# Seven products of a tile: two PSUM chains of one bank each, read between the products, in place of four banks read in four groups

## Chip, cores and metric

The kernel runs on one core of a Trainium2 chip. The metric is device time in microseconds (us) of one execution; before the change its median is 845.22 us over three runs (844.39 to 845.75).

## Reference, cut to what matters

For 8 sequences of 3008 tokens with 256 channels, the first half is a spectral filter (FFT along the sequence, a complex 256x256 matrix, a soft threshold, the inverse FFT). Its result, 24064 tokens by 256, goes through a two-layer block:

```
def _moe_ref(x, w_in, w_out, s, b):      # w_in 256 x 2048, w_out 2048 x 256
    h = x @ w_in
    r = np.maximum(h, 0.0)
    g = s * (r * r) + b
    return (g @ w_out).astype(np.float32)
```

The change concerns the last product alone. Since s and b are scalars, the kernel computes `out = s * (r*r) @ w_out + bias`, where `bias` is b times the column sums of w_out, held in the tile `bias_bc`.

## The kernel before, in words

**Stages.** Each sequence (batch) passes through the filter in stages of small matmuls: stage 1 (tiles x, u), stages 2 and 3 (xf, s, ring, v), stage 4 (vs to yt). The stages' matmuls are cut into units, and `plan` (L1072 to L1118) hangs the units of later batches between the matmuls of the two-layer block of an earlier one. The main loop (L1121 to L1133) runs over token tiles `ti` of up to 512 tokens and, in each, over 16 slots `mc`. A slot emits its planned units, two matmuls of `first_mm` (L847: 512 columns each, into a two-bank tile psh), and then seven or eight matmuls of the *second* layer of the tile before. Every second slot, ScalarE applies the relu to a psh pair (L867, rt<-psh) and ScalarE or VectorE squares it into gt (L877 or L880).

**Who evacuates and squares.** A planner in Python keeps a running load for ScalarE and VectorE (`work`, `act_first`, L175 to L189): each emitted operation adds its cost to its engine, and a free choice (an evacuation in `evac`, a square in `first_mm`) goes to the engine that would be done first. An operation on VectorE that costs less shifts later choices. Each engine executes its own queue in order; the framework adds the waits.

**The seven products.** For 22 of the tiles (`seven`, L1063) the second layer is not done with 8 blocks but with 7 (Winograd's form). The 512 tokens are two halves i, the 2048 hidden channels two halves k (even and odd mc), the 256 outputs two halves j. With a for the squares and B for w_out, VectorE forms s1 = a21+a22 (`s_op` 1), a21 := a11-a21 (`s_op` 3), a11 := a11-s1 (`s_op` 2), and a DMA issued on GpSimd adds the new a11 to a12 (`s_op` 4, L969). Each is done per half q of the hidden dimension. `make_t` (L369) has made four sums T of blocks of w_out. The products, by the numbers that the changed code uses, are

```
1: a11 B11   2: a12 B21   4: a22 T3   5: s1 T0   6: (a11-s1) T1   7: (a11-a21) T2   3: (a12+a11-s1) B22
top left = 1+2;  bottom left = 1+6+7+4;  bottom right = 1+6+7+5;  top right = 1+6+5+3
```

Products 1 and 2 need a11 and a12 as they were, 6 needs `s_op` 2 of both halves, 7 needs `s_op` 3, 5 needs `s_op` 1. A product is 16 matmuls of 128x128 (2 token blocks by 8 channel blocks); the tile's 112 matmuls fill 16 slots of seven. In the first 18 of the 22 tiles products 1 and 2 are interleaved by halves of the channels, in the last four (`alone`, L1045) three are.

**Banks and readout before** (`seven_mms`, L979). The order is 1 2 4 5 6 7 3. A tile takes four banks of 512 floats, with products 1 and 2 in the two halves of one, 4 in one, 5 and 6 in one, 7 and 3 in one. In the first 18 tiles they come from the pool psa with two buffers in turn, in the last four alternately from psa and psf (`sum_bank`, L211). `leave` (L1016) reads them on VectorE in four groups: after 1 and 2 two scalar_tensor_tensor (L1008, `add`) and one tensor_tensor (L1026) that makes a second running sum in `zz` with the other bias; after 4 one; after 5 and 6 one of 256 and one of 512 elements; after 7 and 3 three. The results go to two ost tiles, and SP's queue stores all four at the end. Tiles that are not of the seven kind go through `second_mms` (L918): eight matmuls of 256 columns a slot, one bank for two blocks of 128 tokens, one VectorE readout (L941).

**Order on VectorE around it.** `s_op` 2 and 1 of q=0 and q=1 stand in slot 2 of the products, 3 of q=1 in slot 3, 2 of q=1 in slot 4; `s_op` 1 and 3 of q=0 are emitted one tile earlier, in slots 10 and 11 (L1130).

Of the kernel before, what the change touches and what calls it, by code (L numbers as in the profile page):

```python
# [10 lines left out]
F32 = mybir.dt.float32  # L11
# [85 lines left out]
def kernel(  # L97
# [48 lines left out]
    apool = ctx.enter_context(tc.tile_pool(name="psa", bufs=2, space=bass.MemoryType.PSUM))  # L146
# [66 lines left out]

    def other_bank():
        return apool.tile([P, 512], F32, name="psa", tag="psa")
# [146 lines left out]
    b_21 = cpool.tile([P, P], F32, name="b_21")  # L362
# [6 lines left out]
    def make_t(i):  # L369

        if not T_s:
            nc.vector.tensor_tensor(
                out=b_21, in0=bias_bc[:, P:D], in1=bias_bc[:, 0:P], op=ALU.subtract
            )
            T_s.append(x2pool.tile([P, 4, MC // 2, P], F16, name="T_s", tag="x2"))
# [603 lines left out]
    def seven_mms(ti):  # L979

        tl = tiles[ti]
        size = sub_size(tl)
        hold = {}
        left = [(0, 0), (0, 1), (1, 1), None, (0, 0), (1, 0), (0, 1)]
        firsts = (0, 2, 3, 5)
        T = T_s[0]
        right = [w_block(0, 0), w_block(1, 0), T[:, 3], T[:, 0], T[:, 1], T[:, 2], w_block(1, 1)]

        def mm(n, j, c):

            if n in firsts and j == 0 and c == 0:
                hold["ps"] = sum_bank(ti).rearrange("p (n j e) -> p n j e", n=2, j=2)
            if j == 0 and c == 0:
                hold[n] = hold["ps"][0:size, 0 if n in firsts else 1]
            q, g = divmod(c, 4)
            at = slice(j * size, (j + 1) * size)
            if left[n] is None:
                lhs = sums[(ti, q)][:, g, at]
            else:
                lhs = gts[(ti, q)][:, left[n][0], left[n][1], g, at]  # L1000
            matmul(
                hold[n][:, j], lhs, right[n][:, c],
                start=(n in firsts and j == 0 and c == 0), stop=(c == MC // 2 - 1),
# [3 lines left out]
        def add(out, of, other):  # L1007
            nc.vector.scalar_tensor_tensor(  # L1008
                out=out, in0=of, scalar=s_bc[0:size], in1=other, op0=ALU.mult, op1=ALU.add
            )  # L1010
            work("dve", 0.4)

        def wide(t):
            return t[0:size, 0:P].unsqueeze(1).to_broadcast([size, 2, P])

        def leave(group):  # L1016
            if group == 0:
                hold["z"] = zpool.tile([P, 2, 2, P], F32, name="zz", tag="zz")
            if group in (0, 3):
                hold["o", group] = opool.tile([P, 2, D], F32, name="ost", tag="ost")  # L1020
            z = hold["z"][0:size]
            top = hold["o", 0][0:size]
            if group == 0:
                add(z[:, 0], hold[0], wide(bias_bc))
                add(top[:, :, 0:P], hold[1], z[:, 0])
                nc.vector.tensor_tensor(out=z[:, 1], in0=z[:, 0], in1=wide(b_21), op=ALU.add)  # L1026
                work("dve", 0.34)
            elif group == 1:
                add(z[:, 0], hold[2], z[:, 0])
            elif group == 2:  # L1030
                add(z[:, 1], hold[3], z[:, 1])
                two = hold[4].rearrange("p j e -> p (j e)").unsqueeze(1).to_broadcast([size, 2, D])
                zs = z.rearrange("p h j e -> p h (j e)")
                add(zs, two, zs)
                work("dve", 0.27)
            else:
                for h in range(2):
                    add(hold["o", 3][0:size, :, h * P : (h + 1) * P], hold[5], z[:, h])
                add(top[:, :, P:D], hold[6], z[:, 1])
                for i in range(2):  # L1040
                    for j in range(2):
                        store(tl, 2 * (1 - i) + j, hold["o", 3 * (1 - i)][:, j, :])
# [122 lines left out]
```

## Time and profile before

| what | value |
|---|---|
| median of three runs | 845.22 us (844.39 to 845.75) |
| the profiled execution's own time | 843.5 us |
| its span, first to last instruction | 841.7 us |
| mean granted TensorE clock | 0.999 |
| PE busy | 823.0 us (98% of the span), 7710 matmuls |
| weight loads (PEld) | 599.3 us (71%) |
| VectorE (DVE) busy | 718.2 us (85%), 1120 instructions |
| ScalarE (ACT) busy | 722.1 us (86%), 959 instructions |
| GpSimd (POOL) busy | 87.7 us (10%) |
| readouts of the seven products (L1008 and L1026) | 198 instructions |

How to read it: an engine's busy time is the time in which it had an instruction running. Matmuls overlap each other, so a busy PE may still have waited between two starts. A view of waits gives, for an engine and tile, what ended its idle time. The timeline gives start and length of each instruction, equal neighbours merged, with the idle time ahead of it in brackets.

### The profile page before, as it was taken

Reading aid. Unit: us, or ns where it says so; the run is one execution under the profiler, and the core shown is the slowest. Engines: PE = TensorE matmul, PEld = TensorE weight load, DVE = VectorE, ACT = ScalarE, POOL = GpSimd, SP = SyncE. Lnnn points to the kernel's source line nnn. Section 1 sums busy time; section 2 is a strip of 40 time slices with the busy share of each in tenths; the row PEclk is TensorE's granted clock in tenths of the full one; section 3 lists DMA queues with packets and bytes.
Section 4 is the critical chain, followed back from the end, with each engine's and each line's share of the span. In section 5 each row is a group of like instructions: output and inputs, shape, how many; then the busy total and the mean of one; then the engine's idle time right before and its main releaser. Section 6 shows DMA issues by size and latency. Waiting matters only on the chain.

```text
span 841.7 us, 19681 instructions
## 1 busy us (share of the span) xinstructions
PE 823.0 (98%) x7710; PEld 599.3 (71%) x7710; DVE 718.2 (85%) x1120; ACT 722.1 (86%) x959; POOL 87.7 (10%) x116
## 2 busy tenths in 40 slices
PE   8999999999999999999999999999999999999997
PEld 7857767777677767776677666777667767767765
DVE  5988989998898888888888888788889888879885
ACT  5998988998899988988899888889879898788882
POOL 4550001110010001100010000100001000001000
PEclk9999999999999999999999999999999999999999
DMA  8954587356873478436773458614565253513322
GB/s 199 180 152 102 124 195 193 63 104 151 202 177 66 107 173 215 105 90 143 188 184 70 96 137 206 168 53 108 131 175 142 51 109 99 144 45 76 71 64 62
DMA packets 116959, 107.70 MB, mean 128 GB/s; under 512 B 12806, under 2 KB 100874, under 8 KB 115522
## 3 DMA queue, kind: packets, MB, share of 16 engines
q1 hardware_dynamic: 102498, 80.55, 33.7%
q0 software_dynamic: 14368, 25.89, 19.4%
q8 instruction: 60, 0.98, 0.5%
q14 instruction: 33, 0.27, 0.1%
HBM read 53.52 MB, written 46.66 MB: 119 GB/s over the span
## 4 chain that ended last, share of the span: by engine, by line
PE 70%; DVE 11%; ACT 8%; DMA 6%; issue 3%; SPq 1%; POOL 0%; DVEq 0%; ACTq 0%; POOLq 0%
PE psh L175 29%; PE psa L175 25%; PE psf L175 15%; ACT rt L867 3%; DVE gt L880 2%; DVE gt L976 2%; ACT gt L877 2%; DMA vd<-v 1%; DMA ring<-ring 1%; DMA x<-in_x_dram 1%; DVE ring L699 1%; DMA vs<-vd 1%; PE psm L175 1%; DMA gt<-gt 1%; DVE s L976 1%
## 5 line engine op out<-in xcount | busy, mean ns | idle before, releaser
L867 ACT ACTIVATE rt<-psh 128x1024 f32<-128x1024 f32 (+2 forms) x384 | 387.0, 1009 | 66.5 <-PE psh L175 64.3
L175 PEld LDWEIGHTS <-gt 128*128 128x128 f16 (+1 forms) x3728 | 305.1, 101 | 167.7 <-DMA gt<-gt 1.2
L175 PE MATMUL psh<-yt,w_in 128*128 128x512 f16 (+1 forms) x1344 | 396.6, 378 | 0.1
L880 DVE TENSOR_TENSOR gt<-rt 128x1024 f16<-128x1024 f32 (+2 forms) x238 | 285.2, 1203 | 61.1 <-ACT rt L867 59.7
L175 PE MATMUL psa<-w_out_t,gt 128*128 128x256 f16 (+3 forms) x2432 | 305.9, 252 | 1.0 <-DMA gt<-gt 1.0
L877 ACT ACTIVATE gt<-rt 128x1024 f16<-128x1024 f32 (+2 forms) x146 | 151.7, 1039 | 3.5
L175 PEld LDWEIGHTS <-w_in 128*128 128x128 f16 x1536 | 136.2, 98 | 25.3 <-issue 2.6
L175 PE MATMUL psa<-T_s,gt 128*128 128x128 f16 (+1 forms) x992 | 83.4, 219 | 0.0
L969 POOL DMA_DIRECT2D gt<-gt x44 | 39.7, 902 | 379.7 <-DVE s L976 200.3
L699 DVE TENSOR_TENSOR ring<-psf,s 128x512 f16<-128x512 f32 x84 | 57.5, 685 | 3.5 <-PE psf L175 2.7
L187 ACT CAST u<-psf 96x512 f16<-96x512 f32 x91 | 52.6, 580 | 9.1 <-PE psf L175 8.9
L187 ACT CAST v<-psf 128x512 f16<-128x512 f32 x82 | 47.5, 582 | 11.1 <-PE psf L175 11.1
L175 PEld LDWEIGHTS <-xf 128*128 128x128 f16 x504 | 46.5, 98 | 8.7 <-DVE xf L672 1.9
L175 PE MATMUL psh<-tail,w_in 128*128 128x512 f16 (+1 forms) x192 | 52.1, 353 | 0.0
L175 PE MATMUL psf<-W_g,xf 128*128 128x256 f16 x336 | 50.4, 272 | 1.0 <-ACT xf L187 1.0
L234 POOL DMA_DIRECT2D x<-in_x_dram x36 | 19.2, 538 | 265.2 <-PE psf L175 264.1
L187 ACT CAST yt<-psf 128x470 f16<-128x470 f32 (+2 forms) x84 | 43.3, 534 | 4.1 <-PE psf L175 2.9
L1008 DVE SCALAR_TENSOR_TENSOR ost<-psa,s_bc,zz 128x256 f32<-128x256 f32 (+1 forms) x84 | 38.1, 479 | 7.2 <-PE psa L175 6.5
L941 DVE SCALAR_TENSOR_TENSOR ost<-psa,s_bc,bias_bc 128x512 f32<-128x512 f32 (+2 forms) x49 | 35.6, 726 | 6.9 <-PE psa L175 5.0
L175 PE MATMUL psf<-x,A_t 94*96 94x512 f16 x102 | 38.9, 381 | 2.0 <-ACT v L187 0.8
L175 PE MATMUL psf<-C_t,vs 96*128 96x94 f16 (+1 forms) x484 | 37.9, 205 | 0.8 <-DMA vs<-vd 0.8
L187 ACT CAST xf<-psf 128x512 f16<-128x512 f32 x62 | 36.2, 584 | 2.1 <-PE psf L175 1.9
(118 smaller groups left out, 810.7 us busy)
## 6 DMA issues: line engine op xcount, KB each, us to landing
out_dram<-ost SPq DMA_DIRECT2D x152, 128.0 KB
ud<-u SPq DMA_DIRECT2D x56, 192.0 KB
us<-ud SPq DMA_DIRECT2D x28, 384.0 KB
vd<-v SPq DMA_DIRECT2D x42, 256.0 KB
vs<-vd SPq DMA_DIRECT2D x14, 768.0 KB
x<-in_x_dram POOLq DMA_DIRECT2D x28, 376.0 KB, 6.1
gt<-gt POOLq DMA_DIRECT2D x40, 256.0 KB, 4.4
ring<-ring SPq DMA_DIRECT2D x280, 32.0 KB
```

The lines of the kernel that those rows point to most:

```text
L175: return nc.tensor.matmul(out, lhs, rhs, **how)
L187: return None, nc.scalar.copy(out=dst, in_=src)
L234: nc.gpsimd.dma_start(out=t[0:N1, i * w : (i + 1) * w], in_=xv[:, c * XCH * D + i * w : c * XCH * D + (i + 1) * w],)
L699: nc.vector.tensor_tensor(out=ring[0][:, i % 4], in0=ps, in1=hold[i // 2][:, i % 2].unsqueeze(1).to_broadcast([P, 2, D]), op=ALU.add,)
L867: nc.scalar.activation(out=rt[:, :, 0:w], in_=ps[:, :, 0:w], func=AF.Relu)
L877: nc.scalar.activation(out=gt, in_=rr, func=AF.Square)
L880: last_square[0] = nc.vector.tensor_tensor(out=gt, in0=rr, in1=rr, op=ALU.mult)
L941: nc.vector.scalar_tensor_tensor(out=ost[0:size, 0:k], in0=ps[0:size, 0:k], scalar=s_bc[0:size], in1=bias_bc[0:size].unsqueeze(1).to_broad ...
L969: nc.gpsimd.dma_start(out=a12, in_=a11, accum_op=ALU.add)
L976: nc.vector.tensor_tensor(out=out, in0=a, in1=b, op=op)
L1008: nc.vector.scalar_tensor_tensor(out=out, in0=of, scalar=s_bc[0:size], in1=other, op0=ALU.mult, op1=ALU.add)
```

## The change

The 112 matmuls of a tile stay, and so do their operands; their order, their banks and their readouts change.

- **Order.** 1 2 6 7 5 4 3 in the first 18 tiles, 1 2 4 6 7 5 3 in the last four. After the interleaved ones every product runs the halves of the channels in turn.
- **Banks.** A product uses half of a bank. In the first 18 tiles one chain, x, gathers 1, 6, 5 and 3 in one bank without clearing it; the other, y, holds 2, then 7 (which clears), then 4 on top of 7. In the last four x gathers 1, 6 and 5, y holds 2 and then 7, and a third bank w holds 4 and then 3. The pool psa becomes two tags of one buffer each, taken in turn by `side`; the flip after y makes the next tile's x take the bank that finishes first.
- **Readout.** `leave(n)` is emitted right after the last matmul of product n, one reading of 256 elements for each product in the first 18 tiles (seven operations), nine in the last four. The tensor_tensor with `b_21`, the 512-element operation and `b_21` itself go. Since a chain goes on in the bank that is being read, the next product of the chain may not start until the reading is done. The bottom results are stored when product 4 (in the last four: 5) is read, the top ones after product 3.
- **Moved.** `s_op` 1 and 3 of q=0 are emitted after the slot's products instead of ahead of them, and in slots 11 and 12 (13 and 14 for the last three tiles).

In the built program VectorE has 162 rows of readouts in place of 198, and 260 squares instead of 238; 21 evacuations have gone from VectorE to ScalarE and 22 squares the other way.

```diff
@@ -143,7 +143,7 @@
 
     cpool = ctx.enter_context(tc.tile_pool(name="consts", bufs=1))
     bigpool = ctx.enter_context(tc.tile_pool(name="big", bufs=1))
-    apool = ctx.enter_context(tc.tile_pool(name="psa", bufs=2, space=bass.MemoryType.PSUM))
+    apool = ctx.enter_context(tc.tile_pool(name="psa", bufs=1, space=bass.MemoryType.PSUM))
     fpool = ctx.enter_context(tc.tile_pool(name="psf", bufs=2, space=bass.MemoryType.PSUM))
     dpool = ctx.enter_context(tc.tile_pool(name="dram", bufs=2, space=bass.MemoryType.DRAM))
     xpool = ctx.enter_context(tc.tile_pool(name="xp", bufs=3))
@@ -211,8 +211,11 @@
     def sum_bank(ti):
         return any_bank() if ti >= mark[B - 1] // MC else other_bank()
 
+    side = [0]
+
     def other_bank():
-        return apool.tile([P, 512], F32, name="psa", tag="psa")
+        side[0] = 1 - side[0]
+        return apool.tile([P, 512], F32, name="psa", tag=f"psa{side[0]}")
 
 
     XCH = 8
@@ -359,7 +362,6 @@
 
 
     w_sum = small[:, 2:4]
-    b_21 = cpool.tile([P, P], F32, name="b_21")
     T_s = []
     last_square = [None]
 
@@ -369,9 +371,6 @@
     def make_t(i):
 
         if not T_s:
-            nc.vector.tensor_tensor(
-                out=b_21, in0=bias_bc[:, P:D], in1=bias_bc[:, 0:P], op=ALU.subtract
-            )
             T_s.append(x2pool.tile([P, 4, MC // 2, P], F16, name="T_s", tag="x2"))
         t = T_s[0]
         a, b, op = (
@@ -980,84 +979,99 @@
 
         tl = tiles[ti]
         size = sub_size(tl)
+        alone = ti >= mark[B - 1] // MC
+        C = MC // 2
+        T = T_s[0]
+
+
+        of = {
+            1: ((0, 0), w_block(0, 0), "x"), 2: ((0, 1), w_block(1, 0), "y"),
+            4: ((1, 1), T[:, 3], "w" if alone else "y"), 6: ((0, 0), T[:, 1], "x"),
+            7: ((1, 0), T[:, 2], "y"), 5: (None, T[:, 0], "x"),
+            3: ((0, 1), w_block(1, 1), "w" if alone else "x"),
+        }
+        clears = (1, 2, 4, 7, 3) if alone else (1, 2, 7)
         hold = {}
-        left = [(0, 0), (0, 1), (1, 1), None, (0, 0), (1, 0), (0, 1)]
-        firsts = (0, 2, 3, 5)
-        T = T_s[0]
-        right = [w_block(0, 0), w_block(1, 0), T[:, 3], T[:, 0], T[:, 1], T[:, 2], w_block(1, 1)]
 
         def mm(n, j, c):
 
-            if n in firsts and j == 0 and c == 0:
-                hold["ps"] = sum_bank(ti).rearrange("p (n j e) -> p n j e", n=2, j=2)
-            if j == 0 and c == 0:
-                hold[n] = hold["ps"][0:size, 0 if n in firsts else 1]
+            left, right, to = of[n]
+            if to not in hold:
+                hold[to] = sum_bank(ti).rearrange("p (n j e) -> p n j e", n=2, j=2)[0:size, 0]
+                if to == "y" and not alone:
+                    side[0] = 1 - side[0]
             q, g = divmod(c, 4)
             at = slice(j * size, (j + 1) * size)
-            if left[n] is None:
+            if left is None:
                 lhs = sums[(ti, q)][:, g, at]
             else:
-                lhs = gts[(ti, q)][:, left[n][0], left[n][1], g, at]
+                lhs = gts[(ti, q)][:, left[0], left[1], g, at]
             matmul(
-                hold[n][:, j], lhs, right[n][:, c],
-                start=(n in firsts and j == 0 and c == 0), stop=(c == MC // 2 - 1),
+                hold[to][:, j], lhs, right[:, c],
+                start=(n in clears and j == 0 and c == 0), stop=(c == C - 1),
                 skip_group_check=True,
             )
 
-        def add(out, of, other):
+        def add(out, bank, other):
             nc.vector.scalar_tensor_tensor(
-                out=out, in0=of, scalar=s_bc[0:size], in1=other, op0=ALU.mult, op1=ALU.add
+                out=out, in0=hold[bank], scalar=s_bc[0:size], in1=other, op0=ALU.mult, op1=ALU.add
             )
             work("dve", 0.4)
 
-        def wide(t):
-            return t[0:size, 0:P].unsqueeze(1).to_broadcast([size, 2, P])
-
-        def leave(group):
-            if group == 0:
+        def leave(n):
+
+            if n == 1:
                 hold["z"] = zpool.tile([P, 2, 2, P], F32, name="zz", tag="zz")
-            if group in (0, 3):
-                hold["o", group] = opool.tile([P, 2, D], F32, name="ost", tag="ost")
+            if n in (2, 7):
+                hold["o", n] = opool.tile([P, 2, D], F32, name="ost", tag="ost")
             z = hold["z"][0:size]
-            top = hold["o", 0][0:size]
-            if group == 0:
-                add(z[:, 0], hold[0], wide(bias_bc))
-                add(top[:, :, 0:P], hold[1], z[:, 0])
-                nc.vector.tensor_tensor(out=z[:, 1], in0=z[:, 0], in1=wide(b_21), op=ALU.add)
-                work("dve", 0.34)
-            elif group == 1:
-                add(z[:, 0], hold[2], z[:, 0])
-            elif group == 2:
-                add(z[:, 1], hold[3], z[:, 1])
-                two = hold[4].rearrange("p j e -> p (j e)").unsqueeze(1).to_broadcast([size, 2, D])
-                zs = z.rearrange("p h j e -> p h (j e)")
-                add(zs, two, zs)
-                work("dve", 0.27)
-            else:
-                for h in range(2):
-                    add(hold["o", 3][0:size, :, h * P : (h + 1) * P], hold[5], z[:, h])
-                add(top[:, :, P:D], hold[6], z[:, 1])
-                for i in range(2):
-                    for j in range(2):
-                        store(tl, 2 * (1 - i) + j, hold["o", 3 * (1 - i)][:, j, :])
-
-        C = MC // 2
-        alone = ti >= mark[B - 1] // MC
+            bias = [
+                bias_bc[0:size, h * P : (h + 1) * P].unsqueeze(1).to_broadcast([size, 2, P])
+                for h in range(2)
+            ]
+            top, bot = (hold["o", k][0:size] if ("o", k) in hold else None for k in (2, 7))
+            if n == 1:
+                add(z[:, 0], "x", bias[0])
+            elif n == 2:
+                add(top[:, :, 0:P], "y", z[:, 0])
+            elif n == 4 and alone:
+                add(z[:, 1], "w", bias[0])
+            elif n == 6:
+                add(z[:, 1], "x", z[:, 1] if alone else bias[0])
+            elif n == 7:
+                add(z[:, 0], "y", bias[1])
+            elif n == 5:
+                add(bot[:, :, P:D], "x", z[:, 0])
+            elif n == 3:
+                add(top[:, :, P:D], "w" if alone else "x", z[:, 1] if alone else bias[1])
+                for j in range(2):
+                    store(tl, j, top[:, j, :])
+            if n == (7 if alone else 4):
+                add(bot[:, :, 0:P], "y", z[:, 1])
+            if n == 5 and alone:
+                add(z[:, 1], "x", bias[1])
+            if n == (5 if alone else 4):
+                for j in range(2):
+                    store(tl, 2 + j, bot[:, j, :])
+
+        turns = [1, 2, 4, 6, 7, 5, 3] if alone else [1, 2, 6, 7, 5, 4, 3]
         early = 3 if alone else 2
         order = [
-            (n, j, c) for h in range(2) for n in range(early) for j in range(2)
+            (n, j, c) for h in range(2) for n in turns[:early] for j in range(2)
             for c in range(4 * h, 4 * h + 4)
         ]
-        order += [(n, j, c) for n in range(early, 6) for j in range(2) for c in range(C)]
-        order += [(6, j, c) for h in range(2) for j in range(2) for c in range(4 * h, 4 * h + 4)]
+        order += [
+            (n, j, c) for n in turns[early:] for h in range(2) for j in range(2)
+            for c in range(4 * h, 4 * h + 4)
+        ]
         slots = [[] for _ in range(MC)]
         for at, what in enumerate(order):
             slots[at // 7].append(lambda w=what: mm(*w))
+            if what[1:] == (1, C - 1):
+                slots[at // 7].append(lambda n=what[0]: leave(n))
         for at, n, q in ((2, 2, 0), (2, 1, 1), (2, 4, 0), (3, 3, 1), (4, 2, 1), (5, 4, 1)):
             at += alone and at > 3
             slots[at].append(lambda n=n, q=q: s_op(ti, n, q))
-        for at, group in ((4 + alone, 0), (6, 1), (11, 2), (15, 3)):
-            slots[at].append(lambda group=group: leave(group))
         return slots
 
     def seven(ti):
@@ -1127,10 +1141,12 @@
                 for u in plan.pop(ti * MC + mc, []):
                     u()
                 first_mm(ti, mc)
-                if mc in (10, 11) and seven(ti):
-                    s_op(ti, 1 if mc == 10 else 3, 0)
             for u in nxt[mc]:
                 u()
+            if ti < ti_n and seven(ti):
+                at = 13 if ti > mark[B - 1] // MC else 11
+                if mc in (at, at + 1):
+                    s_op(ti, 1 if mc == at else 3, 0)
     assert not plan
 
 
```

## Prediction

> **What bounds the kernel.** I read the page's busy times and clock, then the waits, then the timeline.
>
> ```profile
> PE 823.0 (98%) x7710; PEld 599.3 (71%) x7710; DVE 718.2 (85%) x1120; ACT 722.1 (86%) x959; POOL 87.7 (10%) x116
> ...
> PEclk9999999999999999999999999999999999999999
> ```
>
> PE is busy throughout at full clock, but busy matmuls overlap, so I walked the starts of all 7710 in the trace. Where nothing waits, a matmul starts 0.216 us after one of 512 columns, 0.109 after 256, 0.056 after 128. By these steps the starts fill 807 of the 836 us from first to last. The other 29 are waits: 7.9 lie in the first 80 us, which the change hardly touches, some 14 in the 22 tiles with seven products. PE is the bound, so a wait of PE comes almost whole onto the end, and no work of PE goes away. What can be won is in its own waits:
>
> ```profile
> engine line waited for: us in total, times, longest us
> PEld L175 <- issue: 7.3, 20, 0.7
> PEld L175 <- DVE ost L1008: 3.5, 7, 1.5
> PEld L175 <- DVE xf L672: 1.9, 6, 0.4
> ...
> PE psa L175 <- DVE ost L1008: 2.3, 5, 1.0
> PE psf L175 <- DVE ring L699: 1.8, 5, 0.5
> ```
>
> These are two answers, weight loads and matmuls, from 80 us on. PE waits for readouts on DVE (the reader is to see `ost L1008`); by starts these waits are eight, always ahead of product 5 (T_s,s), 0.19 to 1.16 us and 3.85 in all. Product 5 takes the bank of 1 and 2 and so needs their second reading.
>
> **Part 1: operations on DVE.** The tile view gives 0.478 us for a 256-element reading, 0.748 for the one of 512, 0.416 for the tensor_tensor. A tile had 7 x 0.478 + 0.748 + 0.416 = 4.51. In the first 18 tiles it will have 7 x 0.478 = 3.35, in the last four 9 x 0.478 = 4.30: 18 x 1.16 + 4 x 0.21 = 21.7 us less. The planner spends part of it: by the built order of the changed kernel 22 squares come to DVE (1.20 each, from ACT at 1.04) and 21 evacuations go to ACT (0.58, from 0.68). DVE ends 21.7 - 26.4 + 14.3 = 9.6 us lighter, ACT 10.7. Neither is the bound: worth 0 by itself, hidden under PE's stream. If they were the bound it would be some 10.
>
> The Trainium skill ("VectorE: DVE Perf Modes", Rules for kernel authors) says to minimize the number of DVE operations. The row speaks otherwise here, DVE being 85% busy beside a full PE; by the rule alone the sum would be up to -21.7 us. A rule against the change: "PSUM — Partial Sum Buffer", Summary: rules for kernel authors, says to read PSUM from another bank than the one that matmuls run into. If none of the new readings were covered, it would be 162 x 0.478 = 77 us, an estimate from that rule and the reading's row.
>
> **Part 2: the wait that goes.** Product 5 gets its bank late no more: -3.85 us, at the places of the eight waits.
>
> **Part 3: the waits that come.** In the first 18 tiles only two banks are left, so a product waits for the reading of the one before last. Between lie 16 matmuls, 2.3 slots, 1.9 to 2.6 us; at product 6 only 8, about one slot, since 1 and 2 are interleaved. Besides, 6 has moved from matmul 80 to 32, and its second half (matmul 40) needs `s_op` 2 of q=1, which DVE does in slots 4 to 5. Behind a late reading in DVE's queue stand that `s_op`, squares and the ring evacuations, for which PE's other units wait. I lay DVE's new order on the recorded times, tile by kind; DVE's next instruction starts some 0.08 before the row of the last ends, PE follows a reading by 0.05 to 0.07.
>
> *Second tile of a pair (starts 146, 248, 338, 440, 644 us).* The rows of before at 440:
>
> ```profile
> 440.89 1.23 DVE L880 TENSOR_TENSOR gt<-rt 128x1024 f16<-128x1024 f32 x1
> 441.21 1.02 ACT L867 ACTIVATE rt<-psh 128x1024 f32<-128x1024 f32 x1 [0.35 <-PE psh L175]
> ...
> 444.15 0.33 PE L175 MATMUL psa<-T_s,gt 128*128 128x128 f16 x3
> ...
> 444.32 0.85 PE L175 MATMUL psf<-W_t,xf 128*128 128x256 f16 x4
> 444.43 0.28 DVE L672 TENSOR_TENSOR xf<-xf 128x256 f16<-128x256 f16 x1
> ```
>
> The matmuls at 444.15 stand where product 6 will start. DVE's new order is square 440.9 to 442.1, two `s_op` to 443.3, a second square (on ACT before; its relu ends 442.24) to 444.45, two xf sums to 444.85, and only then the reading of product 1, to 445.3. Product 6 starts 0.95 late, then waits some 0.17 at matmul 40 (`s_op` 3, a reading and `s_op` 2: 446.95). A wait of 0.24 for xf at 444.4, in the row of 0.85, is swallowed: +0.9.
>
> *First tile of a pair (130, 232, 321, 424, 628).* At 424 a square ends at 428.11, the reading of 1 at 428.5; product 6 was to start at 428.47: +0.1. `s_op` 3, the reading of 2 and `s_op` 2 end at 430.13, matmul 40 is due at 429.66: +0.5. The wait of 0.19 ahead of product 5 goes: +0.4. Product 3 may wait a further 0.4 behind a square and the moved `s_op`; I leave that to the range.
>
> *Tiles at 180, 372, 474, 575.* At 372 the reading of 1 ends at 376.89, product 6 is due at 376.64: +0.3. The reading of 2 then stands ahead of the ring evacuation as one did before, so PE's wait for ring (0.62) shrinks to 0.5. DVE's second half loses 1.16 us, but the xf at its end follows ACT: +0.1.
>
> *The others.* 163: seven operations come ahead of the reading, 1.6 late, 0.7 goes: +0.9. 678: 0.9 late, 1.16 goes: -0.3. 527 and 727: as a first of a pair, 0.6 come and 0.4 go: +0.2 each. Last four: three banks of four in turn leave 16 to 48 matmuls; only matmul 56 meets `s_op` 2, 0.1 late: +0.1 each.
>
> The sum is 5 x (0.9 + 0.4) + 4 x 0.1 + 0.9 - 0.3 + 2 x 0.2 + 4 x 0.1 = **+8.3 us**; the waits that go are in it. Moved `s_op` 1 and 3 are counted where they delay readings; the DMA that follows `s_op` 2 is issued up to 1 us later on POOL, is 4.4 us from issue to landing, and its a12 is needed only by product 3, some 9 us after: 0, or up to 1.2 (the one wait for gt, 1.2 us) where x loads are ahead of it on POOL. SP stores the bottom results one product earlier: 0 (the DMA engines are some half busy there). Against the profiled execution's 843.5 (span 841.7 and 1.8 around it) the sum is 851.8; that execution lies 1.7 below the median 845.22, so I predict 853.5 for the median.
>
> **Bounds.** The new waits at products 7, 5, 4 and 3 have no row of before: 0 below, and above the mean of the eight known waits, 0.48, in 13 tiles more: +6, so 859.5. Below nothing: a lighter DVE and ACT could take away the waits for ost, ring and xf (3.85 + 1.8 + 1.9) and add none: 837.7. I take 0 for them, nearest to the replayed tiles, where DVE arrives with 0.5 us or more to spare at most of those products.
>
> **Rivals.**
> - *Readings in time, faster.* If DVE reaches the reading of product 1 before product 6 is due, only the 3.85 us go: 841.4. For it: 9.6 and 10.7 us less work. Against: in six tiles a square or ring work stands ahead of the reading. It decides at 0.9 us earlier in the second tiles, 0.5 in the first. 18%.
> - *Come and gone cancel*, new waits of 3.9 us: 845.2. 9%. That the change doesn't do what it says can be left out but for the nine readings in the last four tiles.
> - *Every boundary late.* If the lateness of one reading passes to the next, the other products wait too, the +6 above or more: 860. For it: DVE is 87 to 89% busy in these stretches (windows 371 to 392 and 424 to 459), in order. Against: PE's wait gives DVE time to catch up. 13%.
> - Forecast, 848 to 858: 60%.
>
> The range 842 to 859.5 leaves out half of the faster case and most of the last. Faster by over 0.2% (about what a measurement of this kernel can tell from no change, 1.7 us): 0.18; within: 0.09; slower: 0.73.
>
> **What would show it.** Right: no wait ahead of T_s,s any more; new waits of PE for the zz reading right after the interleaved products, near 1 us in the five second tiles; waits for gt (`s_op`) eight matmuls later; 162 readings of 0.48. Wrong: these tiles as long as before (16.2 us at 440), or longer waits at products 7, 5, 4, 3, or PE waiting on psh, whose relu on ACT now shares with 21 more evacuations.

## The result and the profile after

The changed kernel takes 851.08 us (median of five runs, 849.11 to 853.63); the kernel before, run beside it on the same chip, 844.39 (843.89 to 845.75). The ratio is 1.0078, interval 1.0056 to 1.0101: slower by 6.7 us. The profiled execution of the changed kernel took 853.63 us (span 851.5), 10.1 more than that of before. Each kernel of this study has one trace, and the changed kernel's is of the slowest of its five executions: what is read from it accounts for the 10.1 us, of which 6.7 stand between the medians.

The page of the changed kernel, busy times and clock:

```profile
PE 826.2 (97%) x7710; PEld 599.4 (70%) x7710; DVE 709.7 (83%) x1084; ACT 712.5 (84%) x958; POOL 87.5 (10%) x116
...
PEclk9999999999999999999999999999999999999999
```

DVE is 8.5 us lighter and ACT 9.6, as the diff meant, and the kernel is slower. The number of matmuls and the clock have not moved, so what has grown is PE's waiting. The waits of the weight loads from 80 us on (total, times, longest, as before):

```profile
engine line waited for: us in total, times, longest us
PEld L175 <- issue: 13.5, 35, 0.9
PEld L175 <- DVE gt L975: 3.8, 11, 0.5
PEld L175 <- DVE xf L671: 2.9, 5, 0.9
```

And those of the matmuls:

```profile
PE psa L175 <- DVE zz L1016: 4.7, 12, 0.8
PE psf L175 <- DMA vs<-vd: 2.1, 2, 1.7
PE psf L175 <- DVE xf L671: 1.8, 4, 0.6
```

The rows `ost L1008` of before are gone. Two new ones stand in their place: the reading of product 1 (`zz L1016`, the bank) and the new a11 (`gt L975`, `s_op`). "issue" is time for which the profile shows no releaser; it grew from 7.3 to 13.5 us together with the waits of the matmuls that the loads stand behind.

I walked the starts of all matmuls of each profiled execution and added up what each came later than its predecessor's column count allows. Positions are matmuls of a tile's 112. The difference between the execution's own time and the sum of its waits is the last row:

| us | before | after |
|---|---|---|
| ahead of product 5 (T_s,s) | 3.8 | 0 |
| at matmul 32 (product 6 starts) | 0 | 7.2 |
| at matmuls 40 to 47 (its second half) | 0 | 3.3 |
| other products | 1.1 | 2.1 |
| planned units inside the tiles | 7.5 | 10.0 |
| between the tiles, from 80 us on | 5.3 | 4.9 |
| the first 80 us | 11.4 | 11.2 |
| all waits | 29.0 | 38.8 |
| own time less all waits | 814.5 | 814.8 |

(By this walk every small gap counts, so the first 80 us hold 11.4 us rather than the 7.9 of the larger ones alone.) The last row is 814.5 to 814.9 in all fourteen profiled executions of this study, while their times run from 843.1 to 853.6. That is bookkeeping rather than a finding: the 7710 matmuls are the same in all, their column counts add up to 807.0 us, and 7.4 to 7.8 us lie outside the first and the last start. Its use is that a theory about the time has to say where a wait is.

**How a wait at matmul 32 looks.** The second tile of a pair in the changed kernel, timeline (start, length, what, and in brackets the idle time ahead of it):

```profile
448.59 0.68 DVE L975 TENSOR_TENSOR gt<-gt,s 128x1024 f16<-128x1024 f16 x1
...
449.19 0.69 DVE L975 TENSOR_TENSOR s<-gt 128x1024 f16<-128x1024 f16 x1
...
449.80 1.22 DVE L879 TENSOR_TENSOR gt<-rt 128x1024 f16<-128x1024 f32 x1
...
450.93 0.49 DVE L671 TENSOR_TENSOR xf<-xf 128x256 f16<-128x256 f16 x2
...
451.27 0.39 PE L175 MATMUL psf<-W_t,xf 128*128 128x256 f16 x2 [0.40 <-DVE xf L671]
451.34 0.48 DVE L1016 SCALAR_TENSOR_TENSOR zz<-psa,s_bc,bias_bc 128x256 f32<-128x256 f32 x1
...
451.87 0.33 PE L175 MATMUL psa<-T_s,gt 128*128 128x128 f16 x3 [0.20 <-DVE zz L1016]
```

Two `s_op`, a square and the xf sums stand ahead of the reading of product 1, which ends at 451.82; product 6 starts 0.05 us later. One late square makes PE wait twice here: for xf, in a unit that stands ahead of product 6, and then for the bank. The five tiles of this kind have 0.2 to 0.8 us of the first and, in four of them, 0.4 to 0.9 of the second.

The first tile of a pair:

```profile
429.60 0.75 DVE L940 SCALAR_TENSOR_TENSOR ost<-psa,s_bc,bias_bc 128x512 f32<-128x512 f32 x1 [2.02 <-PE psa L175]
...
433.09 1.22 DVE L879 TENSOR_TENSOR gt<-rt 128x1024 f16<-128x1024 f32 x1
...
434.23 0.48 DVE L1016 SCALAR_TENSOR_TENSOR zz<-psa,s_bc,bias_bc 128x256 f32<-128x256 f32 x1
...
434.76 0.33 PE L175 MATMUL psa<-T_s,gt 128*128 128x128 f16 x3 [0.40 <-DVE zz L1016]
...
435.61 0.68 DVE L975 TENSOR_TENSOR gt<-gt,s 128x1024 f16<-128x1024 f16 x1
...
436.35 0.29 PE L175 MATMUL psa<-T_s,gt 128*128 128x128 f16 x2 [0.30 <-DVE gt L975]
```

Here DVE had stood idle for 2.02 us, five operations before the reading, until PE had filled the bank of a readout of the ordinary second layer (L940). The same place in the changed kernel (first view) and in the kernel before (second):

```profile
428.26 1.06 ACT L876 ACTIVATE gt<-rt 128x1024 f16<-128x1024 f32 x1
...
429.69 1.02 ACT L866 ACTIVATE rt<-psh 128x1024 f32<-128x1024 f32 x1
...
430.74 1.23 DVE L879 TENSOR_TENSOR gt<-rt 128x1024 f16<-128x1024 f32 x1 [0.39 <-ACT rt L866]
```

```profile
422.54 1.22 DVE L880 TENSOR_TENSOR gt<-rt 128x1024 f16<-128x1024 f32 x1 [0.68 <-ACT rt L867]
...
423.49 1.02 ACT L867 ACTIVATE rt<-psh 128x1024 f32<-128x1024 f32 x1
...
423.88 0.75 DVE L941 SCALAR_TENSOR_TENSOR ost<-psa,s_bc,bias_bc 128x512 f32<-128x512 f32 x1
```

The readout itself is not late: it starts 0.23 us ahead of the tile's first product matmul in both kernels. What has changed is the square ahead of it. Before, DVE did it; now the planner has given it to ACT (at 428.26), DVE is idle in its place, and ACT's next relu starts 0.14 us ahead of that matmul instead of 0.62. DVE's next square needs this relu, so from there on DVE's queue is 0.48 us late. The time lost comes back as a wait of PE for the bank and one for `s_op` 2.

### The profile page after: what moved, and what is told of

Same layout as the page of the kernel before. It is cut to its first block, busy times and chain, and to the rows that moved or that the text cites. A ratio compares the mean times of both kernels' runs of the same rounds, so it can differ in the third digit from the quotient of the medians.

```text
span 851.5 us, 19686 instructions
## 1 busy us (share of the span) xinstructions
PE 826.2 (97%) x7710; PEld 599.4 (70%) x7710; DVE 709.7 (83%) x1084; ACT 712.5 (84%) x958; POOL 87.5 (10%) x116
## 5 line engine op out<-in xcount | busy, mean ns | idle before, releaser
L879 DVE TENSOR_TENSOR gt<-rt 128x1024 f16<-128x1024 f32 (+2 forms) x260 | 311.3, 1201 | 73.3 <-ACT rt L866 71.8
L175 PE MATMUL psa<-w_out_t,gt 128*128 128x256 f16 (+3 forms) x2480 | 311.6, 252 | 0.9 <-DMA gt<-gt 0.7
L876 ACT ACTIVATE gt<-rt 128x1024 f16<-128x1024 f32 (+2 forms) x124 | 129.3, 1043 | 2.7
L187 ACT CAST yt<-psf 128x470 f16<-128x470 f32 (+2 forms) x95 | 49.5, 528 | 7.3 <-PE psf L175 4.9
L187 ACT CAST v<-psf 128x512 f16<-128x512 f32 x79 | 45.7, 582 | 10.9 <-PE psf L175 10.9
L940 DVE SCALAR_TENSOR_TENSOR ost<-psa,s_bc,bias_bc 128x512 f32<-128x512 f32 (+2 forms) x49 | 35.9, 732 | 20.2 <-PE psa L175 18.4
L187 ACT CAST xf<-psf 128x512 f16<-128x512 f32 x75 | 44.0, 587 | 7.8 <-PE psf L175 7.7
L175 PE MATMUL psf<-ring,T_t 128*128 128x256 f16 x168 | 32.5, 272 | 2.7 <-DMA ring<-ring 1.1
```

What stands on the lines that cost most here:

```text
L175: return nc.tensor.matmul(out, lhs, rhs, **how)
L187: return None, nc.scalar.copy(out=dst, in_=src)
L876: nc.scalar.activation(out=gt, in_=rr, func=AF.Square)
L879: last_square[0] = nc.vector.tensor_tensor(out=gt, in0=rr, in1=rr, op=ALU.mult)
L940: nc.vector.scalar_tensor_tensor(out=ost[0:size, 0:k], in0=ps[0:size, 0:k], scalar=s_bc[0:size], in1=bias_bc[0:size].unsqueeze(1).to_broad ...
```

## The experiments

All ratios are to the kernel before, run beside it on the same chip, with a 95% interval. "Waits" are from the walk of the starts in each kernel's one trace.

### Taking the two waits away

*The reading of product 1 does not touch the bank (first 18 tiles).* It takes a bias tile instead, so product 1 is missing from the top left result.

```diff
-            if n == 1:
+            if n == 1 and not alone:
+                nc.vector.scalar_tensor_tensor(
+                    out=z[:, 0], in0=bias[1], scalar=s_bc[0:size], in1=bias[0], op0=ALU.mult, op1=ALU.add
+                )
+                work("dve", 0.4)
+            elif n == 1:
                 add(z[:, 0], "x", bias[0])
```

> In the first 18 tiles of seven products the reading after product 1 takes its input from the bias tile in SBUF and not from the bank, so product 6 need not wait for it; VectorE still does an operation of that size at that place. Left out: product 1's own part of the top left result. Theory (the loss is two waits of PE inside product 6: 7.3 us at its first matmul for the reading of product 1, 3.2 us at its second half for the s_op 2 that stands behind that reading in VectorE's queue): most of the first wait only moves to the second half, since VectorE is no earlier; 1 to 3 us less than the changed kernel, 848 to 850. Rival A (the loss is in the planner's new choices between ScalarE and VectorE): no change, 851. Rival B (reading a bank that a chain goes on in is the whole loss): 7 us less, 844.

Measured: 850.16 us, ratio 1.0069 (1.0052 to 1.0087), just above the theory's range. The waits at matmul 32 went from 7.2 us to 0, those at 40 from 3.3 to 6.7. The matmuls' and then the weight loads' waits for `s_op`:

```profile
PE psa L175 <- DVE gt L975: 4.0, 9, 0.7
```

```profile
PEld L175 <- DVE gt L975: 6.8, 13, 0.9
```

In the changed kernel they were 1.3 and 3.8. PE came to matmul 40 earlier and met `s_op` 2 of q=1, whose place in DVE's queue had not moved. Most of the wait only changed its place.

*The second half of product 6 does not need `s_op` 2.* It takes a22 in place of the new a11 in half q=1, so a part of product 6 is another one.

```diff
+                if n == 6 and q == 1 and not alone:
+                    left = (1, 1)
                 lhs = gts[(ti, q)][:, left[0], left[1], g, at]
```

> In the first 18 tiles the second half of product 6 multiplies a22 in place of the a11 that s_op 2 makes, so it waits for no s_op. Left out: the right operand of that half of product 6. Theory: the waits at matmul 40 go, 3.2 us, and the first wait stays: 847.5 to 848.5. Rival A (planner): 851. Rival B (bank reading alone): 850 to 851.

Measured: 849.43 us, 1.0058 (1.0035 to 1.0080), 0.9 above the theory's range. The waits at 40 went to 0, those at 32 stayed, 7.6 us.

*Both edits together.*

> Both edits: product 6 waits neither for the reading of product 1 nor for s_op 2. Left out: what the two leave out. Theory: both waits go, 10.4 us, while the 3.85 us of waits ahead of product 5 stay away: 841 to 843, faster than the kernel before. Rival A (planner): 849 to 851. Rival C (every boundary of the chains is late): the waits pass to products 7, 5, 4 and 3, 846 to 850.

Measured: 844.39 us, 0.9995 (0.9979 to 1.0011). Both waits are 0, and the whole loss is gone. The two edits alone bring the ratio down by 0.0009 and 0.0020, which the intervals do not tell from nothing, together by 0.0083: only the pair is the loss. A miss all the same, for it is not the gain that the theory gave: at matmul 48 there are now 2.3 us (0.7 in the changed kernel), above all ahead of product 7 in the tiles at 163 and 678, and at matmul 104 1.9 (1.0) in two tiles, for the DMA of `s_op` 4. With product 5's waits gone and the two new ones gone as well, PE still waits 28.6 us, as much as before (29.0).

### Work on DVE

*The kernel before with less work on DVE*: the tensor_tensor with b_21 left out and the 512-element operation cut to 256, its planner charges kept, so no choice moves. Parts of the bottom right and top right results are missing.

```diff
-                nc.vector.tensor_tensor(out=z[:, 1], in0=z[:, 0], in1=wide(b_21), op=ALU.add)
...
-                add(z[:, 1], hold[3], z[:, 1])
-                two = hold[4].rearrange("p j e -> p (j e)").unsqueeze(1).to_broadcast([size, 2, D])
-                zs = z.rearrange("p h j e -> p h (j e)")
-                add(zs, two, zs)
+                add(z[:, 1], hold[3], wide(bias_bc))
+                add(z[:, 0], hold[4], z[:, 0])
```

> The kernel before without the tensor_tensor that adds b_21 and with the 512-element operation cut to 256, the planner charged as before. Left out: the second running sum's start and product 6's part of it. VectorE does 22 x (0.42 + 0.27) = 15 us less, its order as before. Theory (VectorE's load is no bound): 0 to 1.5 us less, 843 to 844.4. Rival D (the number of operations on VectorE is a bound): 4 us or more less, 840.

Measured: 844.73 us, 1.0008 (0.9989 to 1.0026). Its page:

```profile
PE 823.4 (98%) x7710; PEld 601.1 (71%) x7710; DVE 705.0 (84%) x1098; ACT 722.6 (86%) x959; POOL 88.0 (10%) x116
```

13.2 us of DVE's work are gone, and neither the time nor the waits ahead of product 5 (3.8 us) have moved.

### The planner's choices and the moved s_op, each alone

*The changed kernel with the choices of before* (103 of the first 822 differ):

```diff
+    chosen = list(bin(CHOICES_OF_BEFORE)[3:])
...
-        return max(load["act"], ready) + ta <= max(load["dve"], ready) + td + lean[0]
+        return chosen.pop(0) == "1"
```

> The changed kernel, with each of the planner's 822 choices between ScalarE and VectorE (evacuations and squares) taken from a list of those that the kernel before made; 103 differ. Everything is computed. Theory: the two waits stay; only what the squares ahead of the reading in the second tiles of a pair and VectorE's idle time ahead of the first tiles cost goes, 0 to 4 us: 847 to 851. Rival A (planner): 5 to 7 us less, 844 to 846.

Measured: 850.28 us, 1.0066 (1.0046 to 1.0086). In the first tiles at 424 and 628 the waits at 32 and 40 are now 0.09 and 0.35 us instead of 0.57 and 0.47; in all they are 5.1 and 2.6. But 1.8 us between the tiles (W_g,xf) that the new choices had removed are back.

*The kernel before with the new choices*, by the same edit:

> The kernel before, with each of the planner's 822 choices taken from a list of those that the changed kernel made. Everything is computed. Theory (the loss is two waits inside product 6): the kernel before has no such waits and slack for later readings, 0 to 2 us more: 844 to 847. Rival A (the planner's new choices are the loss): 5 us or more, 850.

Measured: 849.5 us, 1.0058 (1.0040 to 1.0076). That is a miss: the choices alone cost 4.9 us. Its profile has 5.1 us more of waits: 1.1 ahead of product 5, 1.0 at matmul 104, 0.6 at 96, 1.4 in the W_t,xf units, 1.2 in those of ring, 1.0 in those of vs, 0.7 between the tiles for x, against 1.6 less there for W_g,xf and smaller ones both ways. No single place carries it. (The medians are 5.8 apart; 4.9 is by the ratio.) This run also settles where the 2.02 us of idle DVE come from. The `s_op` stand at their old places here, and yet the square ahead of the tile at 424 is on ACT (at 424.01) and DVE idles 2.02 us ahead of the readout; the changed kernel with the choices of before has neither.

*The kernel before with `s_op` 1 and 3 of q=0 moved as in the change*:

```diff
-                if mc in (10, 11) and seven(ti):
-                    s_op(ti, 1 if mc == 10 else 3, 0)
             for u in nxt[mc]:
                 u()
+            if ti < ti_n and seven(ti):
+                at = 13 if ti > mark[B - 1] // MC else 11
+                if mc in (at, at + 1):
+                    s_op(ti, 1 if mc == at else 3, 0)
```

> One part of the change alone: the kernel before with s_op 1 and 3 of q=0 emitted after the slot's products and in slots 11 and 12 (13 and 14 for the last three tiles). Everything is computed. Theory: worth nothing by itself, within 1 us of 844.4. Rival E (the moved operations push the readings of the next tile back): 2 us or more slower.

Measured: 847.72 us, 1.0046 (1.0028 to 1.0065), where the theory had nothing. The waits ahead of product 5 grew from 3.8 to 5.6. Its timeline in a first tile:

```profile
425.77 0.75 DVE L941 SCALAR_TENSOR_TENSOR ost<-psa,s_bc,bias_bc 128x512 f32<-128x512 f32 x1 [2.02 <-PE psa L175]
426.91 1.22 DVE L880 TENSOR_TENSOR gt<-rt 128x1024 f16<-128x1024 f32 x1 [0.39 <-ACT rt L867]
...
432.15 0.48 DVE L1008 SCALAR_TENSOR_TENSOR zz<-psa,s_bc,bias_bc 128x256 f32<-128x256 f32 x1
```

The planner's choices were not held in this run, and they moved as well: DVE has 231 squares in place of 238 and is 8.7 us lighter, ACT 8.1 heavier. So the 4.0 us are the price of the moved operations together with the choices that they drew with them; what they cost by themselves was not measured. The 2.02 us of idle DVE are here too, with the same origin: the square ahead of the readout is on ACT (at 424.43), the next relu comes 0.48 us later in its tile than before, and the reading 0.46.

*The changed kernel with the choices of before and `s_op` 1 and 3 one slot earlier* (10 and 11, still behind the products; a full return was not run):

```diff
-                at = 13 if ti > mark[B - 1] // MC else 11
+                at = 12 if ti > mark[B - 1] // MC else 10
```

> The changed kernel with the choices of the kernel before forced (measured alone: 850.28) and with s_op 1 and 3 of q=0 one slot earlier, in slots 10 and 11, still behind the slot's products. Nothing is left out. Theory (the boundary of 8 matmuls itself is the cause, the lateness of DVE behind moved operations a small part): waits at matmuls 32 and 40 of 6 to 8 us together stay, 849 to 850.5. Rival A (moved s_op make the readings late; that move alone cost the kernel before 4 us): waits at 32 and 40 of under 4 us together, 846 to 848. Rival B (s_op 1 now waits for PE to finish product 5's first half and holds up DVE): 851 to 853, DVE waiting for PE ahead of L975.

Measured: 849.97 us, 1.0062 (1.0043 to 1.0082), waits at 32 and 40 of 5.1 and 2.6. So in the changed kernel the choices and the place of the moved operations are not what makes the two waits: without the 2.02 us of idle DVE, 7.7 us of them remain.

### Where else the wait can go

*`s_op` 2 and 4 of q=1 one slot later, in the kernel before*, to let the readings pass:

```diff
-            at += alone and at > 3
+            at += at > 3
```

> The kernel before, with s_op 2 of q=1 and the DMA after it one slot later in the first 18 tiles, as it is in the last four, so that the readings of products 1 and 2 stand ahead of it on VectorE. Everything is computed. Theory (those readings and not the number of operations set the eight waits of 3.85 us ahead of product 5): each reading is 0.6 us earlier, 2 to 3.5 us less: 841 to 842.5. Rival D (the number of operations on VectorE sets them): no change, 844.4.

Measured: 844.2 us, 1.0010 (0.9986 to 1.0035): a miss. The order on DVE changed in three first tiles, whose waits of 0.2 to 0.3 us went; at 527, 678 and 727 `s_op` 2 still stood ahead of both readings, at 130 between them as before, and 3.3 of 3.8 us stayed. At 163 it did leave, and the wait was 0.79 us instead of 0.73. The choices were not held here either: DVE has five squares more.

*The changed kernel in the order 2 1 7 6 4 5 3*, product 3 clearing y, eight readings (core of the edit):

```diff
-        turns = [1, 2, 4, 6, 7, 5, 3] if alone else [1, 2, 6, 7, 5, 4, 3]
+        turns = [1, 2, 4, 6, 7, 5, 3] if alone else [2, 1, 7, 6, 4, 5, 3]
...
-        clears = (1, 2, 4, 7, 3) if alone else (1, 2, 7)
+        clears = (1, 2, 4, 7, 3) if alone else (1, 2, 7, 3)
```

> The changed kernel with the first 18 tiles in the order 2 1 7 6 4 5 3, chain y holding 2, then 7 (clears), 4 on top, then 3 (clears), chain x 1, 6, 5; eight readings instead of seven, s_op 1 and 3 of q=0 in slots 13 and 14. Nothing is left out. Product 7 stands at matmul 32 and needs the reading of 2 and s_op 3; product 6 stands at 48, where s_op 2 has long been done. Theory (two waits, each for its own cause): the wait at matmul 32 stays, 6 to 8 us in all, the one at 40 (3.3 us) goes: 848 plus or minus 1.5. Rival A (the wait at 40 only moves, as in the run without the reading's wait): 850 to 852, with 2 to 4 us of waits at 40 or 48. Rival B (the eighth reading and the later s_op cost more than the wait): 852 to 855.

Measured: 847.79 us, 1.0037 (1.0023 to 1.0051), within the theory's range but not by its sum: the wait at 40 went (0.1), the one at 32 fell to 3.0, and 4.8 us came at matmuls 0 and 8, where a tile waits for the last readings of the one before. The choices were not held.

*The kernel before with other pairs in a bank*: 1 and 2, 4 and 5, 6, 7 and 3; choices kept.

```diff
-        firsts = (0, 2, 3, 5)
+        firsts = (0, 2, 4, 5)
...
                 add(z[:, 0], hold[2], z[:, 0])
-            elif group == 2:
                 add(z[:, 1], hold[3], z[:, 1])
+            elif group == 2:
...
-        for at, group in ((4 + alone, 0), (6, 1), (11, 2), (15, 3)):
+        for at, group in ((4 + alone, 0), (9, 1), (11, 2), (15, 3)):
```

> The kernel before, order 1 2 4 5 6 7 3 and 9 readings kept, planner's choices kept by force; only the pairing in banks changes: 1 and 2 share a bank, 4 and 5 the next, 6 has one alone, 7 and 3 the last. So product 6 (matmul 64) and not product 5 (matmul 48) takes the bank of 1 and 2, with 32 matmuls between instead of 16. 4 and 5 are read together after product 5. Nothing is left out. Theory (PE pays for a reading that is late in DVE's queue, so distance in matmuls is worth it): the 3.85 us of waits ahead of product 5 go, product 7 finds its bank read 16 matmuls after product 5 with up to 0.5 us of waits in all: 840 to 841.5 beside 844, ratio 0.995 to 0.998. Rival A (any boundary of 16 matmuls is late as often): waits of 2 us or more ahead of product 7, 843 to 846. Rival B (another reading's place makes ring, xf and s_op late): 845 to 848 with longer waits in the units.

Measured: 847.87 us, 1.0041 (1.0026 to 1.0056). A miss: the 3.8 us ahead of product 5 are 0, but 5.2 have come ahead of product 7, as rival A had it. The time lies in rival B's range, and 4.6 us more of waits stand in the vs units, where PE waits for a DMA. (The trace is of the slowest of the twelve executions, 850.65 us.) The timeline ahead of such a wait:

```profile
439.77 1.22 DVE L882 TENSOR_TENSOR gt<-rt 128x1024 f16<-128x1024 f32 x1 [1.73 <-ACT rt L869]
...
441.10 0.69 DVE L978 TENSOR_TENSOR s<-gt 128x1024 f16<-128x1024 f16 x1
441.70 0.48 DVE L1010 SCALAR_TENSOR_TENSOR zz<-psa,s_bc,zz 128x256 f32<-128x256 f32 x1
...
442.10 1.21 DVE L882 TENSOR_TENSOR gt<-rt 128x1024 f16<-128x1024 f32 x1
443.23 0.47 DVE L1010 SCALAR_TENSOR_TENSOR zz<-psa,s_bc,zz 128x256 f32<-128x256 f32 x1
...
443.76 0.38 PE L175 MATMUL psa<-T_s,gt 128*128 128x128 f16 x4 [1.10 <-DVE zz L1010]
```

By the starts product 4 was full at 437.0 and 5 at 439.85. Their readings (441.70 and 443.23) stand behind a square and an `s_op`, and a second square has come between them. Ahead of the first square DVE is idle for 1.73 us, waiting for ACT's relu: the reading of 4 would have fitted into the gap, but the queue is in order.

*Pairs 1 and 2, 4 and 5, 6 and 7, and 3 alone*, which leaves 32 matmuls at all boundaries but the one to the next tile:

```diff
-        firsts = (0, 2, 3, 5)
+        firsts = (0, 2, 4, 6)
...
-        for at, group in ((4 + alone, 0), (6, 1), (11, 2), (15, 3)):
+        for at, group in ((4 + alone, 0), (9, 1), (13, 2), (15, 3)):
```

> The kernel before with order, number of readings and planner's choices kept, and other pairs in a bank: 1 and 2, 4 and 5, 6 and 7, and 3 alone. 6 and 7 are read together after product 7. Nothing is left out. In the pairing tried before (7 and 3 together) product 7 waited 5.2 us in all for the bank of 4 and 5, 16 matmuls after it was full, behind a square and s_op 1 of q=0 in DVE's queue. Now product 6 (matmul 64) takes the bank of 1 and 2 with 32 matmuls between, product 3 (matmul 96) that of 4 and 5 with 32, the next tile's product 4 that of 3 with 32; only the next tile's product 1 takes a bank, that of 6 and 7, 16 matmuls after it was full, in about half the tiles. Theory (distance in matmuls against the queue ahead of the reading): waits at matmuls 48 and 80 under 0.3 us in all, at matmul 0 of the next tile 0 to 2 us: 840.5 to 843 beside 844.5, ratio 0.995 to 0.998. Rival A (three readings of 1.7 us in a row at the end of the tile are late as the others were): 3 to 5 us of waits at matmul 0, 844 to 847. Rival B (late ring, yt and vs behind the bunched readings): waits in the units longer by 4 us or more, 847 to 850.

Measured: 846.34 us, 1.0019 (0.9999 to 1.0040). Waits at 48 and 80: none. At matmul 0: 3.4 us, which is rival A, and 2.5 instead of 1.2 at matmul 104. The boundary:

```profile
441.01 0.74 DVE L1010 SCALAR_TENSOR_TENSOR zz<-psa,s_bc,zz 128x512 f32<-128x512 f32 x1
441.67 0.34 DVE L191 CAST yt<-psf 128x188 f16<-128x188 f32 x1
...
441.93 1.26 DVE L1010 SCALAR_TENSOR_TENSOR ost<-psa,s_bc,zz 128x256 f32<-128x256 f32 x3
...
442.85 0.57 PE L175 MATMUL psa<-w_out_t,gt 128*128 128x128 f16 x7 [0.41 <-DVE ost L1010]
```

Five arrangements, and in each the readings are waited for at a boundary where only 8 or 16 matmuls lie between a full bank and its reuse: 3.8 us at matmul 48 (before), 7.2 at 32 (after), 3.0 at 32 and 4.8 at 0 and 8 (order 2 1 7 6 4 5 3), 5.2 at 80 and 3.4 at 0 (the two pairings). At the boundaries of 32 matmuls that the pairings made, 64 and 96, there is none. A short boundary is not always waited for: in the changed kernel those of 16 matmuls at 64, 80 and 96 have no wait, and that of 8 at matmul 8, where product 2 takes the bank that a tile of the same kind before it finished last, has 0.1 us in all. What stands in DVE's queue decides. No version that computes everything beats the kernel before.

## Why the prediction was right, and where it was off

The side and the size were right: +8.3 us forecast against the profiled execution, +10.1 measured there, +6.7 between the medians (853.5 forecast, 851.08 measured). The mechanism was right too: the loss is two waits inside product 6, and with both taken out the ratio is 0.9995. That the sum came so near is partly luck, as the terms of part 3 show. The "some 14" us of waits that the prediction read in the 22 tiles are 12.4 by the table above.

**Part 1 (DVE's work, worth 0): right, tested by itself.** DVE fell by 8.5 us (9.6 forecast), ACT by 9.6 (10.7). 13.2 us less on DVE, with the choices held, moved nothing. The rule of the Trainium skill ("VectorE: DVE Perf Modes", Rules for kernel authors) to minimize the number of operations does not show in the time here: by it the sum would have been up to -21.7. What the part left out is that the moved choices (43 in the net count, 103 one by one) have a price of their own that is no sum of durations: 4.9 us in the kernel before.

**Part 2 (-3.85): right.** No wait ahead of product 5 is left. But the study also says that such a wait is not simply won: with both new waits removed the kernel came to 844.39 and not to the 841.4 of the rival "readings in time", since 2.3 us at matmul 48 and others took its place.

**Part 3, tile by tile**, change of the waits inside the tile, profile against profile. *Second tiles of a pair* (+0.9 each, 4.5): 1.12, 0.23, 0.82, 0.76 and 0.76, together 3.7. At 338, 440 and 644 DVE's order was the replayed one, operation for operation. The term that was off is the xf wait of 0.24, "swallowed" by the forecast: in three tiles it grew to 0.56 and the wait for the bank shrank to 0.37. *First tiles* (+0.4 each, 2.0): 4.1. The step that failed is "+0.1" for the reading of 1: 0.57 at 424 and 628. I had laid the new order of the products on the recorded DVE times up to there, and these had changed as well: of the choices that part 1 counts only in sum, one gave ACT the square ahead of the tile, and DVE's queue came 0.48 us late. With the old choices the waits are 0.09 and 0.35, as replayed (0.1 and 0.5). Of the 4.1 us, 1.5 are waits for the vs DMA (232 and 321) that no term had. *180, 372, 474, 575* (+0.1 each): 0.28 and three times 0.22. *163* (+0.9): 0.04; its reading was late by 0.4, not 1.6. *678* (-0.3): -0.1. *527 and 727* (+0.2 each): 0.35 and 0.53. *Last four* (+0.4): 0.7, of which 0.52 are one wait at matmul 48 in the tile at 767, for the reading of product 1; it stood behind two `s_op`, and the forecast had only `s_op` 2 at matmul 56. The sum is 10.2 against 8.3 forecast; the second tiles and 163 came out 1.7 below their terms, the first tiles 2.1 above, and part of the errors cancel.

**Bounds.** The waits at products 7, 5, 4 and 3 were taken as 0 and are: 0.65 at matmul 48, of which 0.52 is in the last four, 1.0 at 104 (1.2 before), none at 64, 80 and 96. That refutes "every boundary late". The argument, that PE's wait at 32 gives DVE the time to catch up, fits the run without the two waits, where 2.3 us came at 48. "Come and gone cancel" had 3.9 us of new waits; there were 10.5. The rule of the skill ("PSUM — Partial Sum Buffer", Summary: rules for kernel authors) is to read another bank than the one that matmuls run into. The prediction set it against the change, with an estimate of 77 us if no reading were covered. 7.2 us of waits at the reading were seen, a tenth; while a reading runs, the matmuls of the other chain fill another bank, as the rule asks, so it does not speak against this layout.

**What stays open.** The parts do not add up. Choices alone cost 4.9, moved `s_op` with the choices that they drew along 4.0, and all of it together 6.7; undoing the choices in the changed kernel gives back only 0.0012 of the ratio, less than the intervals tell from nothing. Taking both waits away gives back all. The reading that fits is that late DVE is met by PE once, at whichever boundary is short, so that two causes of lateness share one wait; the runs are consistent with it, and why 103 choices cost 4.9 us by themselves was not taken apart further. Nor was the growth of the vs waits (1.2 to 5.8 us over the traces). And executions of one kernel differ by up to 8.3 us among themselves, at a granted clock of 0.993 to 1.000; with one trace of each, no run here shows which waits make that spread.

## What to carry to other kernels

Where one engine's stream sets the time, count for every buffer that is used again how much of the stream lies between full and reuse, and lay beside it the in-order queue ahead of the reader: here 13.2 us less of work on DVE were worth nothing, and late readings at one boundary made PE wait 7.2 us. A wait that is removed at one boundary can turn up at the next short one, as it did with both pairings, so price a rearrangement by its shortest boundaries and by what stands in the queue there. Replay the reader's queue from far enough back, and the queues that feed it: a square that the planner had given to ACT made ACT's next relu 0.48 us late, and with it DVE's queue up to the reading. When a piece of the change is tried alone, hold the planner's choices, or they move with it.

## What had not been expected of the hardware

Reading one PSUM bank while matmuls fill another cost PE's starts nothing that can be seen. With steps that hold a wait of over 0.03 us left out, a 128-column matmul of the products was followed by the next start after 55.7 ns on average while a 256-element reading of psa ran (260 steps in the changed kernel, 206 in the one before), and after 55.8 and 55.9 ns while no PSUM tile was read. A 256-element reading took 0.47 to 0.49 us in either kernel. Two waits for DMAs differ between the traces though no edit touches these DMAs' sizes: that at matmul 104 in one tile (start 527) for GpSimd's accumulating DMA, from none (`s_op` later) over 1.2 (before) to 2.5 us (pairs 6 and 7), and those in the vs units, from 1.2 to 5.8. Whether the arrangement makes the difference or the single execution, one trace of each cannot tell.
